# Folding two of five product blocks by accumulating DMAs in a dilated-window attention kernel

## The chip, the cores and the metric

The kernel runs on one core of a Trainium2 chip. The metric is device time in microseconds (us): 264.16 us for the kernel before, the median of 3 runs (264.13 to 264.53). The engines are named as in the profile: PE is TensorE's matmuls and PEld its weight loads, DVE is VectorE, ACT is ScalarE, POOL is GpSimd, SP is SyncE, which only issues DMAs.

## The reference

`x` has 2048 rows of 640 columns, bfloat16. It is normalised (`xn`), and two branches are added to it:

```python
xn = layernorm(x)
return x + A(xn, wqkv, wo) + B(xn, w_gate, w_up, w_down)

# A: 32 heads of 20 columns; each position looks at 8 positions, 2 apart, itself and those before
logits = einsum("bhsd,bhswd->bhsw", q, k[gathered]) * 20 ** -0.5     # masked where position < 0
A = (softmax(logits) applied to v[gathered]) @ wo
# B
B = ((xn @ w_gate) * (xn @ w_up)) @ w_down                            # 1536 columns in the middle
```

## The kernel before

The 2048 positions are cut into 4 chunks of 512, and each chunk into 4 tiles of 128 (16 tiles, t = 4c + q). Per chunk:

- layernorm of the tiles (DVE, and one step `rstd` on POOL, L265), transposes into `xnT` (PE for the first four tiles, DMA transposes on SP's queue for the others, L339);
- `qk` (L396): q and k, transposed (columns on partitions, positions along the free side), as five blocks of 128 of the 640 columns. 25 matmuls for q and 25 for k (L405), ACT copies the results to SBUF (L412);
- `vproj` (L430): v per tile (L438, two halves of 5 matmuls), copied by ACT and stored to `vD` in DRAM by a DMA of POOL's queue (L459);
- `prodlog` (L468): for each of the 8 window positions i, DVE multiplies q by the shifted k (L476, 128 x 2560, all five blocks in one instruction). Two window positions share one tile `pw`. The logits are then sums over the 20 columns of a head, and PE makes them: `Ek` is a matrix of zeros and ones (128 x 32 for each block, as a block holds parts of 7 or 8 heads), and for each block i and window position a matmul of 32 output rows (L492) adds that block's part into PSUM. Four window positions stand beside each other in PSUM partitions. A chunk has two such groups of 4 positions x 5 blocks = 20 matmuls;
- ACT copies the logits to SBUF (L505), SP's queue transposes them (L513, `LT`), DVE and ACT make the softmax (L524 to L546);
- `av` (L574): the v rows of a tile's 8 window positions come from `vD` in one DMA of 1280 KB on SP's queue (L556), DVE multiplies and adds (L581 to L596), and SP's queue transposes the result `o` into `oT` (L603). These v tiles and the `pw` tiles share five buffers (tag `pv`);
- `glu` (L614): 24 groups of 5 matmuls (L623), ACT copies, DVE multiplies into `hT` (L639);
- `down` (L651): 12 matmuls of `hT` by `wd` (L664) and 5 of `oT` by `wo` (L667) per half tile, DVE adds x (L674, tile `xr`, loaded by POOL's queue, L648), and the result is stored by POOL's queue (L698).

The order on each engine is not that of the code. Every piece of work is a step of a plan (`Plan`, L32), with an engine, a cost, dependencies and the time it occupies its engine. `order` (L48) plays these costs through, always taking the ready step with the earliest due time, and the program is emitted in that order; each engine then works in order and waits by semaphore. For a step that is a DMA with a size `kb`, the plan lets it end at the start + 2.0 us (or the end of the one before on that engine) plus kb/340. Two attributes matter here: the logits steps (L496) are `urgent`, taken as soon as they are ready, and have a `margin` of 0.9 us, which is added, with `LAG` = 0.06 us, to the end of what they depend on. So a change of one cost moves steps on all engines.

In the order before, PE takes chunk 0's logits between the v matmuls of tile 4 and those of tiles 5 to 7, chunk 1's between q matmuls of chunk 2, chunk 2's in the down stage of chunk 1, and chunk 3's in the down stage of chunk 2. The last chunk's gate and up matmuls (120, of 25.9 us) and its down stage follow after that.

Of the kernel before, what the change touches and what calls it, by code (L numbers as in the profile page):

```python
# [10 lines left out]
ALU = mybir.AluOpType  # L11
# [20 lines left out]
class Plan:  # L32
# [8 lines left out]
    def add(self, eng, cost, fn, deps=(), occ=None, after=(), kb=0):  # L41
        s = Step(eng, cost, fn, deps, occ, after)
        s.kb = kb
        s.idx = len(self.steps)
        self.steps.append(s)
        return s
# [51 lines left out]
def kernel(  # L98
# [11 lines left out]
    nc = tc.nc  # L110
    P = nc.NUM_PARTITIONS
# [4 lines left out]
    H = 32  # L116
    Dh = D // H
# [5 lines left out]
    KT = D // P  # L123
# [4 lines left out]
    CS = CH * P  # L128
    JL = P // H
    NS = D // 2  # L130
    BF, F32 = dt.bfloat16, dt.float32
    assert D == KT * P and F == FT * P and S == NCH * CS and W * H == 2 * P and Dh == JL * KT

    const = ctx.enter_context(tc.tile_pool(name="const", bufs=1))
# [5 lines left out]
    wq = const.tile([P, KT, D], BF, name="wq")  # L140
    wk = const.tile([P, KT, D], BF, name="wk")
# [4 lines left out]
    wd = const.tile([P, FT, D], BF, name="wd")  # L146
    ident = const.tile([P, P], BF, name="ident")
    mhalf = const.tile([P, 1], F32, name="mhalf")
    Ek = const.tile([P, KT, H], BF, name="Ek")
    negm = const.tile([P, 2, HALO], F32, name="negm")  # L150
    vD = dram.tile([HALO + S, D], BF, name="vD")

# [1 line left out]
    add = plan.add  # L154
    T = {}

    def new(key, shape, dtype, tag, bufs, pool=None):
        t = (pool or sb).tile(shape, dtype, name=tag, tag=tag, bufs=bufs)
        T[key] = t
        return t  # L160
# [10 lines left out]
    def wload(dst, src, eng=None):  # L171
        return lambda: (eng or nc.sync).dma_start(out=dst[:], in_=src.rearrange("(i p) f -> p i f", p=P))
# [31 lines left out]

    def consts_e():
        nc.gpsimd.memset(Ek[:], 1.0)
        nc.gpsimd.affine_select(out=Ek[:], in_=Ek[:], pattern=[[P, KT], [-Dh, H]], compare_op=ALU.is_ge,
                                fill=0.0, base=0, channel_multiplier=1)
        nc.gpsimd.affine_select(out=Ek[:], in_=Ek[:], pattern=[[-P, KT], [Dh, H]], compare_op=ALU.is_ge,
                                fill=0.0, base=Dh - 1, channel_multiplier=-1)  # L210

    def consts_m():
        nc.gpsimd.memset(negm[:], 0.0)
# [95 lines left out]
    def pe_main(cost, fn, deps=(), banks=1):  # L309
        nonlocal main  # L310
        waits = []
        for k in range(banks):
            if len(ring) + k >= 6:
                waits.append(ring[len(ring) + k - 6])
        main = add("PE", cost + 0.165, fn, [main, *waits, *deps], occ=cost)
        return main
# [79 lines left out]
    def qk(c, lo, n, rs=(0, 1)):  # L396
        for r in rs:
            for j in range(KT):
                key = ("qk", c, r, j, lo)

                def pe(i0, i1, key=key, r=r, j=j):
                    if i0 == 0:
                        new(key, [P, 512], F32, "ps", 6, psum)
                    for i in range(i0, i1):
                        nc.tensor.matmul(T[key][:, 0:n], lhsT=(wk if r else wq)[:, i, j * P : (j + 1) * P],  # L405
                                         rhs=T["xnT", c][:, i, lo : lo + n], start=(i == 0), stop=(i == KT - 1))

                def ev(key=key, r=r, j=j):
                    if r == 0 and j == 0 and lo == 0:
                        new(("q", c), [P, KT, CS], BF, "q", 2)  # L410
                    dst = T["k", c][:, j, HALO + lo : HALO + lo + n] if r else T["q", c][:, j, lo : lo + n]
                    nc.scalar.copy(dst, T[key][:, 0:n])  # L412

                one = n / 2400 + 0.0027
                ts = range(c * CH + lo // P, c * CH + (lo + n) // P)
                mine = [WK if r else WQ, *[TX.get(t, TT[t]) for t in ts], LASTPW.get(c - 2)]
                if c or r or j:
                    a = pe_main(KT * one, lambda pe=pe: pe(0, KT), mine + [TT[t] for t in ts])
                else:
                    pe_main(3 * one, lambda pe=pe: pe(0, 3), mine)  # L420
                    a = pe_main(2 * one, lambda pe=pe: pe(3, KT), [TT[t] for t in ts], banks=0)
                e = add("ACT", 0.16 + n / 1200, ev, [a, HALOCP[c]], occ=0.07 + n / 1200)
                ring.append(e)
                (Kk if r else Q).setdefault(c, []).append(e)
# [38 lines left out]


    SPLAST = [None]
    PW, LL, LE, SS, DD, AA, O16, OE, V8, DT = {}, {}, {}, {}, {}, {}, {}, {}, {}, {}

    def prodlog(c):  # L468
        for g in range(2):
            for j in range(4):  # L470
                i = 4 * g + j

                def mul(i=i):
                    if i % 2 == 0:
                        new(("pw", c, i // 2), [P, 2, KT, CS], BF, "pv", 5)
                    nc.vector.tensor_tensor(T["pw", c, i // 2][:, i % 2, :, :], T["q", c][:],  # L476
                                            T["k", c][:, :, DIL * i : DIL * i + CS], ALU.mult)

                m = 8 * c + i
                w = [LL.get(2 * c - 1), O16.get(4 * c - 4), O16.get(4 * c - 3), O16.get(4 * c - 2)][i // 2]  # L480
                PW[m] = add("DVE", 1.48, mul, [*Q[c], *Kk[c], w], occ=1.395, after=[PW.get(m - 1) if i else V8.get(4 * c - 1)])
        LASTPW[c] = PW[m]
        if c == 0:
            load_v8(0)
        for g in range(2):
            n = 2 * c + g

            def lg(g=g):
                l = new(("lps", c, g), [P, 512], F32, "pl", 2, psum)
                for i in range(KT):  # L490
                    for j in range(4):
                        nc.tensor.matmul(l[H * j : H * (j + 1), :], lhsT=Ek[:, i, :], rhs=T["pw", c, 2 * g + j // 2][:, j % 2, i, :],  # L492
                                         start=(i == 0), stop=(i == KT - 1), tile_position=(0, H * j),
                                         skip_group_check=True)

            LL[n] = add("PE", 1.25, lg, [PW[m], LL.get(n - 1), LE.get(n - 2), LE.get(n - 1 - g), CE], occ=1.12)  # L496
            LL[n].urgent = True
            LL[n].margin = 0.9

            def ev(g=g):  # L500
                L = new(("L", c, g), [P, CS], BF, "L", 2)
                if c == 0:
                    ps = T["lps", c, g]
                    nc.vector.tensor_tensor(ps[:, 0:HALO], ps[:, 0:HALO], negm[:, g, :], ALU.add)
                nc.scalar.copy(L[:], T["lps", c, g][:])  # L505

            LE[n] = add("ACT", 0.585, ev, [LL[n], SS.get(n - 2), CM], occ=0.5)

            def tr(g=g):
                if g == 0:  # L510
                    new(("LT", c), [P, CH, W, H], BF, "LT", 1)
                out = T["LT", c][:].rearrange("p t (g w) h -> p t g (w h)", g=2)[:, :, g, :]
                nc.sync.dma_start_transpose(out=out, in_=T["L", c, g][:])  # L513

            early = [SPLAST[0]] if c == 0 else []
            SS[n] = SPLAST[0] = add("SP", 3.5, tr, [LE[n], DD.get(2 * c - 1), DD.get(2 * c - 2)], occ=1.25, after=early, kb=160)

# [32 lines left out]
    def load_v8(t):  # L550
        def fn():
            v = new(("v8", t), [P, W, D], BF, "pv", 5)
            r0 = t * P
            src = vD[r0 : r0 + P, :]
            src = bass.AP(tensor=src.tensor, offset=src.offset, ap=[[D, P], [DIL * D, W], [1, D]])
            nc.sync.dma_start(out=v[:], in_=src)  # L556
        order = [SPLAST[0]] if t < CH - 1 else [SS[2 * (t // CH) + 1]] if t % CH in (1, 2) else []
        c, u = divmod(t, CH)
        order.append(V8[t - 1] if u else PW[8 * c + 6])
        if t == 3:  # L560
            order.append(WL["o"])
        w = LL[2 * c + (u - 1) // 2] if u else O16.get(t - 1)
        V8[t] = add("SP", 6.0, fn, [VS[t], VS.get(t - 1), w, CZ], occ=0.5, after=order, kb=1280)
        if t < 3:
            SPLAST[0] = V8[t]
            V8[t].floor = (40.0, 0, 0)[t]

    def load_down():
        WL["d"] = SPLAST[0] = add("SP", 8, wload(wd, B_w_down), after=[SPLAST[0]], occ=0.5, kb=1920)

    def load_out():
        WL["o"] = SPLAST[0] = add("SP", 8, wo_load, after=[SPLAST[0]], occ=2.7, kb=1100)

# [134 lines left out]
    a = st_in(0, 0)  # L708
    a = st_in(0, 1, a)
    aggr_in(0, a)  # L710
    a = st_in(1, 0)
    a = st_in(1, 1, a)
# [10 lines left out]
    a = st_in(2, 0)  # L723
    a = st_in(2, 1, a)
# [6 lines left out]
    a = st_in(3, 0)  # L731
    a = st_in(3, 1, a)
# [9 lines left out]
    CE = add("POOL", 1.2, consts_e, [C0, RS[3]])  # L742
# [77 lines left out]
```

## Time and profile before

| what | value |
|---|---|
| median of the runs | 264.16 us (264.13 to 264.53) |
| span of the profiled execution | 263.0 us, first to last instruction |
| mean granted TensorE clock | 1.000 |
| logits matmuls, L492 | 160 of 128 x 32 by 128 x 512, 380 ns each in the row, four overlap |
| products, L476 | 32 of 128 x 2560, 1484 ns each |
| DMA moved | 46.55 MB, mean 177 GB/s |

The profile shows one execution, and its own time is given by its span; the runs' times hold what lies around it as well. The page gives busy time by engine, the span in 40 slices (a digit is a tenth of the slice), the DMA queues, the chain of work that ended last, and groups of instructions by line. Further views: an engine's waits in total; the chain in order of time; an engine's timeline (start, duration, line); busy time of each engine in a given stretch, with the DMA share; and DMA issues with the median time from issue to landing. Matmuls overlap in time, so 25 of them of 379 ns take 5.39 us in a row.

### The profile page before, as it was taken

What the parts mean: (1) busy time and instruction counts of PE and PEld (TensorE: products, weight loads), DVE (VectorE), ACT (ScalarE), POOL (GpSimd) and SP (SyncE); (2) the same over time, 40 slices, a digit from 0 to 9 for tenths busy, and PEclk for the clock granted to TensorE, in tenths of its full rate; (3) what the DMA queues carried; (4) which work ended last, traced back from release to release, by engine and by line L of the source; (5) the groups of instructions that cost most, each with busy time, mean ns of one, the idle gap of its engine ahead of it and who ended that gap; (6) DMA issues with size and microseconds to landing.
All of it is one profiled execution on the core that took longest, in us unless ns stands there. A gap on an engine that the chain in (4) does not pass through costs nothing.

```text
span 263.0 us, 4102 instructions
## 1 busy us (share of the span) xinstructions
PE 258.2 (98%) x1574; PEld 140.4 (53%) x1574; DVE 214.6 (82%) x337; ACT 106.1 (40%) x197; POOL 39.4 (15%) x84
## 2 busy tenths in 40 slices
PE   7999999999999999999999999999999999999995
PEld 2645445444577546444477554644456764445763
DVE  5586997999999969999999189999992999993221
ACT  3655557655300258455500155655541105554000
POOL 4551036000031021400001000420000004000000
PEclk9999999999999999999999999999999999999999
DMA  7978997999978139931167299451903995111001
GB/s 217 326 175 231 402 373 171 370 362 244 195 155 270 54 68 370 316 114 27 25 125 250 66 311 319 97 150 25 224 3 75 365 293 134 26 25 25 27 25 50
DMA packets 50707, 46.55 MB, mean 177 GB/s; under 512 B 24786, under 2 KB 47840, under 8 KB 50688
## 3 DMA queue, kind: packets, MB, share of 16 engines
q1 hardware_dynamic: 46704, 37.10, 50.0%
q0 software_dynamic: 2384, 8.05, 9.2%
q10 hardware_dynamic: 1600, 1.15, 1.4%
q8 instruction: 12, 0.20, 0.3%
q14 instruction: 7, 0.06, 0.1%
HBM read 35.39 MB, written 5.26 MB: 155 GB/s over the span
## 4 chain that ended last, share of the span: by engine, by line
PE 94%; DMA 3%; DVE 1%; issue 0%
PE ps L623 39%; PE ps L664 20%; PE ps L405 17%; PE ps L667 8%; PE ps L438 7%; PE pl L492 3%; DMA wq<-in_A_wqkv_dram 3%; DMA x<-in_A_x_dram 1%; DVE st L251 1%; DVE xr L674 0%; DVE mv L257 0%; DVE ve L259 0%; DVE x L270 0%
## 5 line engine op out<-in xcount | busy, mean ns | idle before, releaser
L623 PE MATMUL ps<-xnT,wg 128*128 128x512 bf16 x240 | 59.6, 379 | 0.0
L623 PE MATMUL ps<-xnT,wu 128*128 128x512 bf16 x240 | 59.6, 379 | 0.0
L664 PE MATMUL ps<-wd,hT 128*128 128x320 bf16 (+2 forms) x384 | 57.4, 299 | 0.0
L476 DVE TENSOR_TENSOR pv<-q,k 128x2560 bf16<-128x2560 bf16 x32 | 46.5, 1484 | 1.7 <-ACT k L412 1.7
L664 PEld LDWEIGHTS <-hT 128*128 128x128 bf16 x384 | 37.0, 98 | 16.5 <-issue 0.8
L581 DVE TENSOR_TENSOR pv<-pv,a 128x5120 bf16<-128x5120 bf16 x16 | 45.1, 2819 | 0.1
L628 ACT CAST gs<-ps 128x512 bf16<-128x512 f32 x48 | 28.2, 587 | 32.1 <-PE ps L623 32.1
L623 PEld LDWEIGHTS <-wu 128*128 128x128 bf16 x240 | 23.5, 98 | 28.3
L623 PEld LDWEIGHTS <-wg 128*128 128x128 bf16 x240 | 23.5, 98 | 27.7
L628 ACT CAST us<-ps 128x512 bf16<-128x512 f32 x48 | 28.2, 588 | 22.4 <-PE ps L623 21.4
L674 DVE TENSOR_TENSOR xr<-ps,xr 128x320 bf16<-128x320 f32 (+2 forms) x32 | 15.0, 486 | 24.4 <-PE ps L667 16.1
L667 PE MATMUL ps<-wo,oT 128*128 128x320 bf16 (+2 forms) x160 | 27.0, 299 | 0.0
L698 POOL DMA_DIRECT2D out_dram<-xr x14 | 7.6, 545 | 124.6 <-DVE xr L674 118.0
L590 DVE TENSOR_TENSOR pv<-pv 128x2560 bf16<-128x2560 bf16 x16 | 23.8, 1485 | 0.1
L438 PE MATMUL ps<-wv,xnT 128*128 128x320 bf16 x160 | 23.2, 299 | 0.4 <-ACT xnT L351 0.4
L412 ACT CAST q<-ps 128x512 bf16<-128x512 f32 x20 | 11.7, 586 | 28.3 <-PE ps L405 28.3
L639 DVE TENSOR_TENSOR hT<-gs,us 128x512 bf16<-128x512 bf16 x48 | 19.5, 419 | 4.1 <-ACT us L628 4.1
L405 PE MATMUL ps<-xnT,wq 128*128 128x512 bf16 x100 | 22.4, 379 | 0.4 <-DMA wq<-in_A_wqkv_dram 0.4
L405 PE MATMUL ps<-xnT,wk 128*128 128x512 bf16 x100 | 22.2, 379 | 0.0
L438 PEld LDWEIGHTS <-xnT 128*128 128x128 bf16 x160 | 15.3, 98 | 7.4 <-ACT xnT L351 0.5
L667 PEld LDWEIGHTS <-oT 128*128 128x128 bf16 x160 | 15.5, 98 | 6.3
L251 DVE BATCH_NORM_STATS2 st<-x 128x6 f32<-128x320 bf16 x32 | 13.9, 481 | 4.4 <-DMA x<-in_A_x_dram 4.4
(54 smaller groups left out, 177.4 us busy)
## 6 DMA issues: line engine op xcount, KB each, us to landing
pv<-vD SPq DMA_DIRECT2D x16, 1280.0 KB, 9.9
vD<-v_t POOLq DMA_DIRECT2D x16, 160.0 KB, 4.5
xr<-in_A_x_dram POOLq DMA_DIRECT2D x16, 160.0 KB, 3.6
out_dram<-xr POOLq DMA_DIRECT2D x14, 160.0 KB, 3.7
wg<-in_B_w_gate_dram SPq DMA_DIRECT2D x1, 1920.0 KB, 8.1
wu<-in_B_w_up_dram SPq DMA_DIRECT2D x1, 1920.0 KB, 11.9
wd<-in_B_w_down_dram SPq DMA_DIRECT2D x1, 1920.0 KB, 14.6
x<-in_A_x_dram SPq DMA_DIRECT2D x11, 160.0 KB, 6.8
```

Source lines behind the costliest of these rows:

```text
L251: nc.vector.bn_stats(T["st", t][:, g, :], T["x", t][:, g * NS : (g + 1) * NS])
L405: nc.tensor.matmul(T[key][:, 0:n], lhsT=(wk if r else wq)[:, i, j * P : (j + 1) * P], rhs=T["xnT", c][:, i, lo : lo + n], start=(i == 0), ...
L438: nc.tensor.matmul(T["psv", t, n][:, 0:NS], lhsT=T["xnT", c][:, i, q * P : (q + 1) * P], rhs=wv[:, i, n * NS : (n + 1) * NS], start=(i == ...
L476: nc.vector.tensor_tensor(T["pw", c, i // 2][:, i % 2, :, :], T["q", c][:], T["k", c][:, :, DIL * i : DIL * i + CS], ALU.mult)
L581: nc.vector.tensor_tensor(v[:].rearrange("p w (j h) -> p w j h", j=Dh, h=H), v[:].rearrange("p w (j h) -> p w j h", j=Dh, h=H), T["a", n][ ...
L590: nc.vector.tensor_tensor(v[:, 0:4, :], v[:, 0:4, :], v[:, 4:8, :], ALU.add)
L623: nc.tensor.matmul(ps[:], lhsT=(wu if r else wg)[:, i, f * P : (f + 1) * P], rhs=T["xnT", c][:, i, :], start=(i == 0), stop=(i == KT - 1))
L628: nc.scalar.copy(s[:], T[key][:])
L639: nc.vector.tensor_tensor(h[:], T["gs", c, f][:], T["us", c, f][:], ALU.mult)
L664: nc.tensor.matmul(ps, lhsT=T["hT", c, f][:, q * P : (q + 1) * P], rhs=wd[:, f, sl], start=(f == 0), stop=(f == FT - 1 and not wo_part))
L667: nc.tensor.matmul(ps, lhsT=T["oT", t][:, g, :], rhs=wo[:, g, sl], start=False, stop=(g == KT - 1 and f1 == FT))
L674: nc.vector.tensor_tensor(T["xr", t][:, sl], T["psD", t, n][:, 0:w], T["xr", t][:, sl], ALU.add)
```

## The change

The columns of q and k are taken in another order: block j now holds the columns j, j + 5, j + 10 and so on of the 640. As a head has 20 columns and 20 is a multiple of 5, each block holds 4 columns of every head, and partition p belongs to head p // 4 in each of the five blocks. The weights themselves stay as loaded: PE's weight load reads every fifth column. `Ek` becomes one matrix of 128 x 32 for all blocks.

Since a partition has the same head in every block, blocks may be added to each other before the logits. After every second product a new step `fold` does so: POOL issues a DMA with an accumulating destination, which adds the blocks 2 and 3 of a `pw` tile (2 positions x 2 blocks x 512, 512 KB) into its blocks 0 and 1. The logits then sum the blocks 0, 1 and 4: 12 matmuls a group, not 20, and they wait for the folds. The product steps, the softmax and all else keep their code; the order is planned anew.

```diff
-    Ek = const.tile([P, KT, H], BF, name="Ek")
+    Ek = const.tile([P, H], BF, name="Ek")
...
-                        nc.tensor.matmul(T[key][:, 0:n], lhsT=(wk if r else wq)[:, i, j * P : (j + 1) * P],
+                        nc.tensor.matmul(T[key][:, 0:n], lhsT=(wk if r else wq)[:, i, :].rearrange("p (c b) -> p c b", b=KT)[:, :, j],
...
+    LEVELS = (1, 1, 1, 1)
+    FOLDER = ('POOL', 'POOL', 'POOL', 'POOL')
+    LEFT = (tuple(range(KT)), (0, 1, KT - 1), (0, KT - 1), (0,))
+    HALVES = ((0, 2, 2, 4), (0, 1, 1, 2), (0, 1, KT - 1, KT))
+
+    def fold(c, u):
+        s = PW[8 * c + 2 * u + 1]
+        for lo, hi, a, b in HALVES[: LEVELS[c]]:
+            def fn(lo=lo, hi=hi, a=a, b=b):
+                w = T["pw", c, u]
+                if FOLDER[c] == "DVE":
+                    nc.vector.tensor_tensor(w[:, :, lo:hi, :], w[:, :, lo:hi, :], w[:, :, a:b, :], ALU.add)
+                else:
+                    nc.gpsimd.dma_start(out=w[:, :, lo:hi, :], in_=w[:, :, a:b, :], accum_op=ALU.add)
+            n = (hi - lo) * 2 * CS
+            if FOLDER[c] == "DVE":
+                s = add("DVE", 0.25 + n / 1920, fn, [s], occ=0.165 + n / 1920)
+            else:
+                s = add("POOL", 4.0, fn, [s], occ=1.2, kb=n / 4)
+        return s
...
+                if i % 2:
+                    FO[4 * c + i // 2] = fold(c, i // 2)
...
-                for i in range(KT):
+                left = LEFT[LEVELS[c]]
+                for i in left:
                     for j in range(4):
-                        nc.tensor.matmul(l[H * j : H * (j + 1), :], lhsT=Ek[:, i, :], rhs=T["pw", c, 2 * g + j // 2][:, j % 2, i, :],
-                                         start=(i == 0), stop=(i == KT - 1), tile_position=(0, H * j),
+                        nc.tensor.matmul(l[H * j : H * (j + 1), :], lhsT=Ek[:], rhs=T["pw", c, 2 * g + j // 2][:, j % 2, i, :],
+                                         start=(i == left[0]), stop=(i == left[-1]), tile_position=(0, H * j),
                                          skip_group_check=True)
 
-            LL[n] = add("PE", 1.25, lg, [PW[m], LL.get(n - 1), LE.get(n - 2), LE.get(n - 1 - g), CE], occ=1.12)
+            took = 0.022 + 0.2195 * len(LEFT[LEVELS[c]])
+            LL[n] = add("PE", took + 0.13, lg, [*[FO[4 * c + u] for u in range(4)], LL.get(n - 1), LE.get(n - 2), LE.get(n - 1 - g), CE], occ=took)
```

In the order that the plan makes of it, chunk 0's logits stand 25 v matmuls later on PE than before, chunk 1's behind all q and k matmuls of chunk 2, chunk 2's between the k matmuls of chunk 3, and chunk 3's behind the first 5 gate matmuls of the last chunk. PE has 64 matmuls fewer, POOL's queue 16 DMAs more. On DVE, chunk 0's products follow each other as before; in the other chunks they mix with other `xr` and `hT` steps than before.

More of the change, by code (lines that the diff above doesn't have):

```diff
@@ L206, in consts_e @@
         nc.gpsimd.memset(Ek[:], 1.0)
-        nc.gpsimd.affine_select(out=Ek[:], in_=Ek[:], pattern=[[P, KT], [-Dh, H]], compare_op=ALU.is_ge,
+        nc.gpsimd.affine_select(out=Ek[:], in_=Ek[:], pattern=[[-JL, H]], compare_op=ALU.is_ge,
                                 fill=0.0, base=0, channel_multiplier=1)
-        nc.gpsimd.affine_select(out=Ek[:], in_=Ek[:], pattern=[[-P, KT], [Dh, H]], compare_op=ALU.is_ge,
-                                fill=0.0, base=Dh - 1, channel_multiplier=-1)
+        nc.gpsimd.affine_select(out=Ek[:], in_=Ek[:], pattern=[[JL, H]], compare_op=ALU.is_ge,
+                                fill=0.0, base=JL - 1, channel_multiplier=-1)
     def consts_m():
@@ L465 @@
     SPLAST = [None]
+    FO = {}
     PW, LL, LE, SS, DD, AA, O16, OE, V8, DT = {}, {}, {}, {}, {}, {}, {}, {}, {}, {}
+    LEVELS = (1, 1, 1, 1)
[17 more added lines that the diff above has]
+        return s
     def prodlog(c):
```

## The prediction

> **What bounds the kernel now.** I read the engine table and the slices first, then TensorE's waits, then the chain of waits in order of time.
>
> ```profile
> PE 258.2 (98%) x1574; PEld 140.4 (53%) x1574; DVE 214.6 (82%) x337; ACT 106.1 (40%) x197; POOL 39.4 (15%) x84
> ...
> PE   7999999999999999999999999999999999999995
> ...
> DMA  7978997999978139931167299451903995111001
> ```
>
> PE is busy in every slice; DVE at 82% is not the limit. PE's waits add up to 2.1 us, all before 12.3 us:
>
> ```profile
> PE ps L242 <- DVE wv L192: 1.3, 1, 1.3
> PE ps L405 <- DMA wq<-in_A_wqkv_dram: 0.4, 1, 0.4
> PE ps L438 <- ACT xnT L351: 0.4, 1, 0.4
> ```
>
> So from 12.23 us to the end the span is a sum of matmuls in a fixed order: a matmul removed comes off one for one, and a new wait in that row goes on one for one. The logits (L492) stand in the chain four times (start, duration):
>
> ```profile
> 35.34 1.36 PE ps L438 x10
> 36.70 2.27 PE pl L492 x40
> 38.97 4.18 PE ps L438 x30
> ...
> 91.85 2.27 PE pl L492 x40
> ...
> 145.89 2.27 PE pl L492 x40
> ...
> 197.05 2.27 PE pl L492 x40
> ```
>
> **1. Matmuls removed: minus 3.6 us.** A chunk's 40 logits matmuls take 2.27 us, 0.057 each; 24 take 1.36. Saved 0.91 in each of 4 chunks, all on the path: 3.6 us.
>
> **2. Strided weight loads: 0.** The 200 loads for q and k now read every fifth column. Such a load shows 98 ns (L405, PEld), beside matmuls that follow each other every 216 ns (25 take 5.39 us). 118 ns may be added before it shows. No row has a strided load: from below nothing can be gained, from above see rival C. I take 0.
>
> **3. The later place of the logits: 0.** In the changed order, chunk 3's logits stand behind the first five gate matmuls of the last chunk, not in the down stage before it. Counted in matmuls of the trace, they end at 213.2 us instead of 199.3. Before, the last `o` (tile 15) ended on DVE at 237.2, 37.8 us after the logits. In between the new order has three more hT products (0.34 each) and six fewer xr additions (0.40): 36.4 us, so 249.6, plus 2.8 for the transpose: 252.4. PE would need it at 254.5 (the old 258.2 less 3.6). 2 us of slack; without them it would be PE's wait, one for one.
>
> **4. The accumulating DMAs.** After every second product GpSimd issues one: 512 KB read from blocks 2 and 3, added into 0 and 1. 16 in all, and the logits wait for them. Products and adds stay as they were on DVE. On POOL's queue an issue is bounded by the 0.55 us of today's issues and twice that, as there are twice the rows (256 of 2 KB, not 128); I take 1.1, by the row count. Behind chunk 0's four stand a vD store and the rstd of tiles 8 and later; the four issues end near 36.3, and before, that store was issued at 37.46, the rstd at 38.02. Nothing is pushed. In chunks 1 to 3 they alternate with stores to out that nobody waits for at once. SP's queue issues nothing new, but its transfers share the DMA engines.
>
> The place that matters is chunk 0. DVE's timeline first, then busy time by stretch (its last two columns are the DMA share and GB/s):
>
> ```profile
> 23.85 11.31 DVE L476 TENSOR_TENSOR pv<-q,k 128x2560 bf16<-128x2560 bf16 x8 [1.68 <-ACT k L412]
> ```
>
> ```profile
> 34.00:36.00 2.00, 2.00 (x14) 1.07 (x12) 2.00 (x4) 1.17 (x3) 0.00 (x0) 1.00 1.02 386
> 36.00:38.00 2.00, 2.00 (x34) 1.01 (x35) 1.93 (x8) 1.00 (x3) 0.54 (x1) 1.00 1.08 365
> 38.00:40.00 2.00, 2.00 (x28) 1.06 (x21) 1.97 (x9) 1.21 (x3) 1.79 (x4) 1.00 0.79 267
> ```
>
> Eight products in 11.31 us: a pair every 2.83, ready at 26.7, 29.5, 32.3 and 35.2. Meanwhile the DMA engines are full (share 1.02 or more from 24 to 38) with wu and the first v load from vD, and free at about 38.5. PE, with 25 more v matmuls (0.136 each) ahead of the logits, reaches them at 36.7 + 3.4 = 40.1, and the half that needs the last two adds at 40.8: 5.6 us after the last product.
>
> What does one add cost the DMA engines? No row shows an accumulating DMA. 512 KB at the 394 to 405 GB/s of 24 to 38 us is 1.3 us as a copy, the lower end. An add must also read its destination: twice the reads make 2.6, and if reads and writes all counted, 3.9, the upper end. [...]
>
> [...]
>
> How such a transfer shares full engines is shown by POOL's own: four xr loads issued together at 44.4, beside SP's loads, and the same four at 219.5, alone:
>
> ```profile
> xr<-in_A_x_dram POOLq DMA_DIRECT2D x4, 160.0 KB, 6.2
> ```
> ```profile
> xr<-in_A_x_dram POOLq DMA_DIRECT2D x4, 160.0 KB, 3.0
> ```
>
> Half as fast: about an equal share. A single 160 KB issue lands after 5.3 us in the full stretch (vD at 25.3) and 2.1 in an idle one (out at 89.6).
>
> Neither side is idle until the work is done, so the sum decides: SP's backlog ended at 38.5; four adds of 2.6 make 10.4 more, so all ends by 48.9. At an equal share from 29.5 (the first add's data) the adds end about there too; with somewhat more than half, at 47.6. PE therefore waits from 40.8 to about 48.3: **7.5 us** (6.8 to 8.1). At 3.9 the sum ends at 54.1: 13.3 us. Behind the waiting matmul stand all of PE's work and, through it, everything else; wu (needed 1 us after the logits) has landed by then, at 43 to 45.
>
> Before the opening matmuls TensorE was idle, and these ten (L242) take 4.45 us, about 0.42 apart against 0.216 later: a cold start loses 2 us. An idle 7.5 us may bring it again: 0 to 2.2, I take 1.5, nearer the one row there is.
>
> **Chunks 1 to 3.** The DMA share is 0.11 to 0.26 from 84 to 96 us. Alone, an add lands after 2.1 (the 160 KB row), less its 0.4 of data, plus 0.5 for the longer issue and 2.6: 4.8. The plan releases the logits 2.0 + 512/340 + 0.06 + 0.9 = 4.5 us after the last product, PE is up to one group (1.1) later, and the half that needs the last add 0.7 after that: 5.2 to 6.3. No wait; at 3.9, up to 0.9 each. The first adds of chunks 2 and 3 overlap a v load (6.8 us, issued at 137.3 before), which may push the last: 0 to 1.5. I take 0.5 in all.
>
> **Sum.** 263.0 - 3.6 + 7.5 + 1.5 + 0.5 = 268.9 us of span. The median of the runs is 264.16, 1.16 above the profiled span: **270.0 us**, 2.2% slower. Less than 0.2% can't be told from no change here.
>
> **Rivals.**
> - **B, the adds run like copies (faster).** At 1.3 us each, four take 5.2 and keep pace with the pairs at half share (2.6 against 2.83). The last lands between 35.2 + 3.5 (idle engines: 2.1 + 0.9 data + 0.5) and 35.2 + 7.1 (the 5.3 row plus 352 KB at half rate): a wait of 0 to 1.5, say 0.8. 263.0 - 3.6 + 0.8 + 1.16 = 261.4 (260.6 to 262.1). For it: nothing measured here says that adding costs more. Against it: the destination must be read. The point between B and my forecast: the logits' wait reaches 3.6 us, at adds of about 1.8 to 2.0 us.
> - **C, the strided loads show.** Beyond 216 ns each ns costs 0.2 us over 200 loads; at three times 98 it is 15.6, so 276 even with B. For it: 10 bytes between columns is new. Against it: 118 ns of cover. [...]
> - **D, in between:** adds of 1.6 to 2.2 us, or more than half a share for POOL: waits of 2 to 5.5, no or little cold start: 262.6 to 267.5, on either side of no change.
>
> **Chances.** Forecast 0.52 (its own range 267.5 to 274.5, with the wait from 6 to 10 and the cold start from 0 to 2.2; adds of 3.9 us would give 277 and are left out); B 0.30; C 0.05; D 0.13. My range reaches from B to the forecast's upper end: 260.9 to 274.5. Faster: B and a little of D, 0.33. Within 0.2%: 0.05. Slower: 0.62.
>
> **What would show it.** PE's waits: a new row "PE pl <- DMA pv<-pv" of about 7.5 us, almost all in chunk 0; in B it is under 1.5. The DMA issues: pv<-pv lands after 4.8 us or so alone, and 9 or more at its longest. L405's weight loads: still 98 ns, or hidden under 216. The chain: 24 logits matmuls in 1.36 us. DVE's last `o` well ahead of PE. It is wrong if the adds land within 5.6 us in chunk 0, or if the wait sits in chunks 1 to 3.

## The result and the profile after

The changed kernel takes 281.96 us, the median of 4 runs (280.57 to 283.04), beside 264.33 (264.13 to 264.53) for the kernel before: a ratio of 1.0664, interval 1.0628 to 1.0701. It is slower by three times what was forecast (270.0), and outside the range (260.9 to 274.5). The profiled execution took 280.57 us, with a span of 278.8. In the experiments below, times, ranges and ratios are of the undisturbed runs; a few runs of e5, e7, e10, e11 and e12 in a slower state (in e12 one of 269.77 us at a mean clock of 0.987, beside a median of 264.82) are left out.

The page of the changed kernel: busy time, TensorE's slices, its granted clock, the DMA engines, POOL's queue (packets, MB, share of 16 engines' span), and the adds from issue to landing.

```profile
PE 260.0 (93%) x1510; PEld 143.5 (51%) x1510; DVE 214.8 (77%) x337; ACT 104.8 (38%) x197; POOL 58.4 (21%) x100
...
PE   7999971999999998999999997999999959999996
...
PEclk9999995799999999999999999999999997999999
DMA  7979999699996997895046995991115997940122
...
q0 software_dynamic: 6736, 16.44, 25.4%
...
pv<-pv POOLq DMA_DIRECT2D x16, 512.0 KB, 7.8
```

PE was busy in every slice before; now it has four holes, one for each chunk, and behind the first and the last the clock is down too (digits 5 and 7 of PEclk, and 7). PE's waits in total (us, times, longest):

```profile
PE pl L517 <- DMA pv<-pv: 14.1, 7, 3.8
PE ps L242 <- DVE wv L192: 1.3, 1, 1.3
PE ps L438 <- ACT xnT L351: 0.4, 1, 0.4
```

One row is new, the one that the prediction named: logits that wait for an add. It holds 14.1 us, and not "almost all in chunk 0". PE's timeline has the seven (start, duration; in brackets the idle time before it):

```profile
39.34 0.39 PE L517 MATMUL pl<-pv,Ek 128*32 128x512 bf16 x2
41.23 0.82 PE L517 MATMUL pl<-pv,Ek 128*32 128x512 bf16 x10 [1.50 <-DMA pv<-pv]
44.89 0.61 PE L517 MATMUL pl<-pv,Ek 128*32 128x512 bf16 x2 [2.83 <-DMA pv<-pv]
49.32 1.46 PE L517 MATMUL pl<-pv,Ek 128*32 128x512 bf16 x10 [3.82 <-DMA pv<-pv]
...
107.63 1.04 PE L517 MATMUL pl<-pv,Ek 128*32 128x512 bf16 x14
109.55 0.82 PE L517 MATMUL pl<-pv,Ek 128*32 128x512 bf16 x10 [0.88 <-DMA pv<-pv]
...
166.69 1.04 PE L517 MATMUL pl<-pv,Ek 128*32 128x512 bf16 x14
169.59 0.82 PE L517 MATMUL pl<-pv,Ek 128*32 128x512 bf16 x10 [1.86 <-DMA pv<-pv]
...
225.68 0.83 PE L517 MATMUL pl<-pv,Ek 128*32 128x512 bf16 x12
226.85 0.39 PE L517 MATMUL pl<-pv,Ek 128*32 128x512 bf16 x2 [0.34 <-DMA pv<-pv]
230.14 1.44 PE L517 MATMUL pl<-pv,Ek 128*32 128x512 bf16 x10 [2.90 <-DMA pv<-pv]
```

A group's ten last matmuls take 0.82 us in chunks 1 and 2, but 1.46 and 1.44 in chunks 0 and 3, at a lowered clock (0.50 granted from 48 to 52 us, 0.57 from 230 to 234). From the first logits matmul of a chunk to the start of the next other work, less the 1.36 us that 24 matmuls need, PE lost 10.0, 1.3, 2.3 and 4.5 us; the matmuls behind chunks 0 and 3, still at the low clock, lost 1.1 and 1.0 more. That is 11.1 + 1.3 + 2.3 + 5.5 = 20.2. With 3.6 removed and a start that was 0.7 earlier (the first logits would have come at 40.0 by the matmuls ahead of them, and came at 39.3), 263.0 + 20.2 - 3.6 - 0.7 = 278.9, beside a span of 278.8: nothing else grew.

### The profile page after: what moved, and what is told of

It reads as the page before. It is cut to its first block, busy times and chain, and to the rows that moved or that the text cites. A ratio compares the mean times of both kernels' runs of the same rounds, so it can differ in the third digit from the quotient of the medians.

```text
span 278.8 us, 4033 instructions
## 1 busy us (share of the span) xinstructions
PE 260.0 (93%) x1510; PEld 143.5 (51%) x1510; DVE 214.8 (77%) x337; ACT 104.8 (38%) x197; POOL 58.4 (21%) x100
## 3 DMA queue, kind: packets, MB, share of 16 engines
q0 software_dynamic: 6736, 16.44, 25.4%
## 4 chain that ended last, share of the span: by engine, by line
DVE 31%; PE 25%; issue 23%; DMA 13%; POOL 5%; ACT 2%; POOLq 0%; DVEq 0%; ACTq 0%
PE ps L649 11%; DMA pv<-pv 8%; DVE pv L607 8%; DVE pv L498 6%; PE ps L690 5%; DVE pv L616 5%; DMA vD<-v_t 4%; PE ps L405 4%; POOL pv L482 3%; DVE hT L665 3%; DVE pv L620 2%; PE ps L438 2%; PE ps L693 2%; DVE xr L700 2%; DVE st L251 1%
## 5 line engine op out<-in xcount | busy, mean ns | idle before, releaser
L649 PE MATMUL ps<-xnT,wu 128*128 128x512 bf16 x240 | 60.7, 384 | 0.0
L498 DVE TENSOR_TENSOR pv<-q,k 128x2560 bf16<-128x2560 bf16 x32 | 46.2, 1481 | 1.7 <-ACT k L412 1.7
L607 DVE TENSOR_TENSOR pv<-pv,a 128x5120 bf16<-128x5120 bf16 x16 | 45.1, 2818 | 0.1
L482 POOL DMA_DIRECT2D pv<-pv x16 | 19.1, 1195 | 48.3 <-issue 25.4
L724 POOL DMA_DIRECT2D out_dram<-xr x14 | 10.3, 737 | 77.4 <-DVE xr L700 77.4
L438 PE MATMUL ps<-wv,xnT 128*128 128x320 bf16 x160 | 23.9, 304 | 0.4 <-ACT xnT L351 0.4
L517 PE MATMUL pl<-pv,Ek 128*32 128x512 bf16 x96 | 9.7, 437 | 14.1 <-DMA pv<-pv 14.1
L444 ACT CAST v_t<-ps 128x320 bf16<-128x320 f32 x32 | 13.2, 429 | 21.7 <-DMA vD<-v_t 17.8
L438 PEld LDWEIGHTS <-xnT 128*128 128x128 bf16 x160 | 15.4, 99 | 8.2 <-issue 1.3
## 6 DMA issues: line engine op xcount, KB each, us to landing
wu<-in_B_w_up_dram SPq DMA_DIRECT2D x1, 1920.0 KB, 17.1
```

The costliest lines, as they stand in the source:

```text
L438: nc.tensor.matmul(T["psv", t, n][:, 0:NS], lhsT=T["xnT", c][:, i, q * P : (q + 1) * P], rhs=wv[:, i, n * NS : (n + 1) * NS], start=(i == ...
L444: nc.scalar.copy(T["v_t", t][:].rearrange("p (j h) -> p j h", j=Dh, h=H)[:, :, n * H // 2 : (n + 1) * H // 2], T["psv", t, n][:, 0:NS].rea ...
L482: nc.gpsimd.dma_start(out=w[:, :, lo:hi, :], in_=w[:, :, a:b, :], accum_op=ALU.add)
L607: nc.vector.tensor_tensor(v[:].rearrange("p w (j h) -> p w j h", j=Dh, h=H), v[:].rearrange("p w (j h) -> p w j h", j=Dh, h=H), T["a", n][ ...
L649: nc.tensor.matmul(ps[:], lhsT=(wu if r else wg)[:, i, f * P : (f + 1) * P], rhs=T["xnT", c][:, i, :], start=(i == 0), stop=(i == KT - 1))
```

## The experiments

Theory after the result: the adding DMAs are the whole loss. Each takes the 16 DMA engines some 2.9 us, they land late, and PE stands. Rivals: the strided weight loads; POOL's issues; other loads beside the adds; the place of the logits in the order; the vector engine (DVE) close behind PE.

### The strided loads, and chunk 0

```diff
-    LEVELS = (1, 1, 1, 1)
+    LEVELS = (0, 0, 0, 0)      # e1_permute_only
+    LEVELS = (0, 1, 1, 1)      # e2_no_fold_chunk0
```

> Only the permuted columns and the one Ek: no block is added to another, the logits sum five blocks as before (LEVELS all 0). Theory: the strided weight loads hide under the 216 ns between matmuls, so this is the kernel before, 264.2 to 264.6 us, and L405's loads still show about 98 ns. Rival (strided loads show): each ns beyond 216 costs 0.2 us; part of the 17.6 us would sit here, 266 or more.

Measured: 264.16 us (264.05 to 264.79), before 264.16; ratio 1.0002, interval 0.9992 to 1.0011. The permuted columns and the single `Ek` cost nothing. A strided load is slower by itself, here in the changed kernel (98 ns before), but 118 ns are still hidden beside matmuls that come every 216:

```profile
L405 PEld LDWEIGHTS <-wk 128*128 128x128 bf16 x100 | 11.7, 118 | 10.1 <-issue 0.4
```

> No adds in chunk 0 (LEVELS 0, 1, 1, 1), all else as in the changed kernel. Theory (adds queue behind each other and behind SP's loads; the waits belong to their chunks): the 11.1 us that chunk 0 loses on PE (10.0 in the wait, 1.1 of slow matmuls after it) go, the 0.9 us saved there come back: 282.0 - 10.2 = 271.8, and PE's waits in chunks 1 to 3 stay at 1.3, 2.3 and 5.5. Rival (the waits of chunks 1 to 3 hang on the delay of chunk 0): they change by more than 1 us each.

Measured: 269.26 us (267.56 to 270.02), ratio 1.0183 (1.0145 to 1.022). Chunk 0's four adds, with the order that goes with them, are worth 12.7 us of the 17.6. Those of the other chunks are dearer than the 0.5 us forecast: with them alone the kernel is 5.1 us slower than before, though 2.7 us of matmuls are gone. The theory's 271.8 was missed, for the waits did not stay: they are 0.8 us in chunk 1, 2.6 in chunk 2 and none in chunk 3, where the new order brings PE to the logits 6.5 us after the last product, and not 5.4.

### Copies instead of adds, and both by themselves

```diff
-                    nc.gpsimd.dma_start(out=w[:, :, lo:hi, :], in_=w[:, :, a:b, :], accum_op=ALU.add)
+                    nc.gpsimd.dma_start(out=w[:, :, lo:hi, :], in_=w[:, :, a:b, :])      # e3_copy
```

> The 16 DMAs copy blocks 2 and 3 over 0 and 1 in place of adding to them: same queue, rows, bytes written and order, but no read of the destination; the output is not the reference's. Theory (the second read makes an add cost about twice a copy): the q0 queue takes some 1.3 us of all engines for each instead of 2.9, chunk 0's last one lands before 43, PE waits less than 3 us in all: 261.4 to 264. Rival (what costs is the issue on POOL's queue, with its 256 rows and its latency): copies land as late as adds, 279 to 283.

Measured: 266.58 us (265.82 to 267.04), ratio 1.0087 (1.0067 to 1.0107). The queue of POOL and the wait at the logits in this run:

```profile
q0 software_dynamic: 4688, 16.44, 17.1%
```
```profile
PE pl L517 <- DMA pv<-pv: 1.6, 1, 1.6
```

The megabytes are the same 16.44 as with adds, the share of the engines is 17.1% of 264.0 us and not 25.4% of 278.8. Less the 24.2 us of the kernel before (9.2% of 263.0), a copy takes (45.1 - 24.2) / 16 = 1.3 us of all engines, an add (70.8 - 24.2) / 16 = 2.9. Same order, same number of issues, 15.4 us apart. The last copy of chunk 0 had landed by 42.1 us, as the theory had it; its time, 261.4 to 264, was missed, and e9 below shows why. POOL's own part differs by 0.5 us an issue (0.72 and 1.20); the engines' part differs by 1.6 us each, 6.4 in a chunk. It is the adding, and not the issue, that costs.

> The DMAs by themselves on idle engines, nothing of the model computed: one add, another, four adds in a row, the same with copies of POOL's queue, then with copies of SP's queue; x is copied to the output. Theory: four adds land 2.1 to 2.9 us apart and four copies 1.2 to 1.5 apart; a single add lands after 4.5 to 5.5 us, a single copy after 3.3 to 4. Rival (issue bound): adds and copies in a row both land 1.2 us apart, as POOL issues them.

A program with nothing of the kernel but such DMAs, on idle engines: one add twice, four adds, one copy twice, four copies, and the copies again from SP's queue. L27 on DVE reads each tile as soon as it has landed, so its starts show the landings:

```profile
24.18 1.36 POOL L36 DMA_DIRECT2D pw<-pw  x1 [23.74 <-DVE pw L27]
29.46 1.80 DVE L27 COPY pw<-pw 128x128 bf16<-128x128 bf16 x8 [5.59 <-DMA pw<-pw]
...
46.62 0.20 DVE L27 COPY pw<-pw 128x128 bf16<-128x128 bf16 x1 [8.62 <-DMA pw<-pw]
49.33 0.19 DVE L27 COPY pw<-pw 128x128 bf16<-128x128 bf16 x1 [2.52 <-DMA pw<-pw]
52.03 1.34 DVE L27 COPY pw<-pw 128x128 bf16<-128x128 bf16 x6 [2.50 <-DMA pw<-pw]
...
53.67 0.75 POOL L39 DMA_DIRECT2D pw<-pw  x1 [10.51 <-DVE pw L27]
56.90 1.80 DVE L27 COPY pw<-pw 128x128 bf16<-128x128 bf16 x8 [3.53 <-DMA pw<-pw]
...
68.75 0.19 DVE L27 COPY pw<-pw 128x128 bf16<-128x128 bf16 x1 [5.20 <-DMA pw<-pw]
70.15 0.20 DVE L27 COPY pw<-pw 128x128 bf16<-128x128 bf16 x1 [1.21 <-DMA pw<-pw]
71.87 1.34 DVE L27 COPY pw<-pw 128x128 bf16<-128x128 bf16 x6 [1.52 <-DMA pw<-pw]
```

Alone, an add is there 5.3 us after its issue began (29.46 - 24.18), a copy after 3.2. In a row adds land 2.7 us apart, copies 1.4 and 1.7, from SP's queue as from POOL's; as POOL issues an add every 1.2 us, the issue is not the bound. An add costs 2.7 / 1.56 = 1.7 copies in a row, and 2.9 / 1.3 = 2.2 by engine time in the kernel. That the read of the destination makes it dearer is not shown here: in the kernel's queue an add also counts 272 packets and a copy 144, and no run separates the two.

### The place of the logits, and the load of v beside the adds

```diff
-                s = add("POOL", 4.0, fn, [s], occ=1.2, kb=n / 4)
+                s = add("POOL", 4.0, fn, [s], occ=1.2, kb=n / 2)      # e5_honest_price
+                s.floor = (41, 42, 46, 50)[u] if c == 0 else 0
...
-            LL[n].margin = 0.9
+            LL[n].margin = 2.4
```

> The planner is told what the adds cost here: 1024 KB of queue time each (3.0 us) instead of 512 KB, 2.4 us of margin ahead of the logits instead of 0.9, and for chunk 0 ends of 41, 42, 46 and 50 us. It then puts 48.7 us of other matmuls ahead of chunk 0's logits instead of 35.1, and 213.4 us instead of 202.6 ahead of the last logits. Theory 1 (the loss is only PE standing at logits that were placed too early): the four waits of 20.2 us go, the 3.6 us of removed matmuls show, 260 to 264 us. Theory 2 (the add stands in a loop of each chunk that the vector engine already fills, products to logits to softmax to products, so a later place only moves the idle time to another wait or to the end): PE waits of at least 8 us stay, at the logits of chunks 1 to 3, at the down projection or at the end, 268 to 280 us. I hold theory 2 for likelier.

Measured: 294.28 us (291.85 to 295.62), 1.114 times the kernel before. PE's waits:

```profile
PE ps L691 <- DVE hT L666: 10.8, 4, 4.0
PE ps L694 <- DMA wo<-in_A_wo_dram: 6.0, 1, 6.0
PE ps L691 <- DVE o L623: 2.5, 1, 2.5
...
PE pl L518 <- DMA pv<-pv: 0.6, 1, 0.6
```

Theory 2 holds in its mechanism, beyond its range of 268 to 280: the logits hardly wait, and much behind them does. The allowances were generous (chunk 0's logits came at 59.7 us and had no wait at all), so the size of the loss is this plan's own; that the wait moved and did not go is what it shows.

```diff
+            if t % CH == 0 and t:      # e6_v_after_adds; in e14_v_after_adds_0: if t == 0, and pw of chunk 0
+                nc.sync.dma_start(out=scr[:], in_=T["pw", t // CH, 3][0:1, 1, 0:2, 0:2])
             nc.sync.dma_start(out=v[:], in_=src)
...
-        order.append(V8[t - 1] if u else PW[8 * c + 6])
+        order.append(V8[t - 1] if u else PW[8 * c + 6] if c == 0 else FO[4 * c + 3])      # e14: if c else FO[3]
```

The plan is told of it too; the order on PE, DVE, ACT and POOL stays that of the changed kernel, and in e6 that on SP changes.

> In chunks 1 to 3 the first load of v (1280 KB) is held back by a transfer of four elements that reads the last added product, so that it starts only when the four adds have landed. Theory A (the adds of chunks 1 to 3 land late since they share the 16 DMA engines with that load): the last adds land 5 to 6 us after their issue, the waits of chunks 2 and 3 fall from 2.3 and 5.5 us to about 1.5 each, 276 to 279 us. Theory B (the adds are late by their own time, issue and engines, and by the products being finished late): the waits stay, 281 to 283 us, or more if the late load of v makes the weighting wait.

Measured: 290.24 us (288.25 to 290.51), ratio 1.0971 (1.0945 to 1.0998). At the logits of chunks 1 to 3 PE waited 0.90, 1.98 and 1.95 us, not 0.88, 1.86 and 3.24: theory B for chunks 1 and 2, theory A for a part of chunk 3 only.

```profile
110.11 0.82 PE L518 MATMUL pl<-pv,Ek 128*32 128x512 bf16 x10 [0.90 <-DMA pv<-pv]
...
174.54 0.82 PE L518 MATMUL pl<-pv,Ek 128*32 128x512 bf16 x10 [1.98 <-DMA pv<-pv]
...
235.67 0.82 PE L518 MATMUL pl<-pv,Ek 128*32 128x512 bf16 x10 [1.95 <-DMA pv<-pv]
```

The late load costs more than it brings; a new row has 7.6 us:

```profile
PE pl L518 <- DMA pv<-pv: 13.2, 6, 4.2
PE ps L693 <- DVE hT L668: 7.6, 5, 2.8
```

> In chunk 0 alone the first load of v (1280 KB) is held back, by a transfer of four elements that reads the last added product, until the four adds have landed; all else as in the changed kernel. Theory (the adds of chunk 0 share the 16 DMA engines with this load, which a window of 400 GB/s moves in 3.4 us, and with the load of the up weights): PE resumes some 2 to 3 us earlier, 278 to 280 us. Rival (the adds and the up weights alone fill the engines until 49 us, the load of v takes its turn behind them): 281 to 283 us.

Measured: 285.17 us (284.04 to 286.43), ratio 1.0793 (1.0757 to 1.0829). In chunk 0 the theory was right: the last ten logits matmuls started at 46.17 and not at 49.32, so 3 us of that wait were the v load's share. At the end it was wrong, as was the rival's number. The first weighting by the softmax (L610, L607 in the changed kernel) began at 60.6 us, beside 61.5: the late load gave back most of the 3 us. Chunk 1's last add landed at 109.2, beside 109.6, and PE, which was there earlier, waited 2.6 us for it and got the low clock behind that (0.57 from 110 to 114 us). PE's earlier start became a longer wait, and the same followed in chunk 2: waits of 0.86 and 2.17 us, with the low clock behind them (digit 5 of PEclk from 171 to 178 us, and ten matmuls in 1.47 us, not 0.82).

### The adds on DVE

```diff
-    FOLDER = ('POOL', 'POOL', 'POOL', 'POOL')
+    FOLDER = ('DVE', 'DVE', 'DVE', 'DVE')      # e7_dve; with LEVELS (1, 1, 1, 0) e10, (1, 1, 0, 0) e11, (1, 0, 0, 0) e12
```

> The same sums by 16 adds on the vector engine instead of 16 DMAs; about 1.2 us each by the 1.48 us that a product of 2560 elements a partition takes, 19 us in all on an engine that is busy for 215 us. The logits keep three blocks. Theory 1 (the loss is the DMA's latency and its share of the DMA engines; the vector engine has 50 us of slack): no wait at the logits, 260 to 264 us. Theory 2 (the vector engine's loop is what sets when logits can be had, slack or not): most of the 19 us show at the end, 270 to 280 us.

Measured: 268.14 us (267.86 to 269.02), ratio 1.0159 (1.0144 to 1.0174); between the two theories. An add takes 1.22 us (DVE's L480), and nothing waits at the logits. PE waits in the last down stage instead, 22.5 and 28.7 us behind the start of the last logits:

```profile
PE ps L690 <- DVE hT L665: 5.1, 2, 2.8
```

> Adds on the vector engine in chunks 0, 1 and 2, none in chunk 3, whose logits keep five blocks. The planner puts 203.7 us of other matmuls ahead of the last logits, 210.2 in the version with adds in every chunk. Theory (with the adds on the vector engine nothing waits at the logits, and what cost time was the tail behind the last logits): three times 0.91 us is gained, 260.3 to 262 us. Rival (the adds fill the vector engine's loop in every chunk, and it is this that shows at the end): 264.5 to 268 us.

> Adds on the vector engine in chunks 0 and 1 only; 196.9 us of other matmuls ahead of the last logits (185.1 in the kernel before). Theory of the tail: twice 0.91 us is gained, 262.0 to 262.8 us. Rival of the loop: 263.5 to 266 us.

> Adds on the vector engine in chunk 0 only; 190.0 us of other matmuls ahead of the last logits. Theory of the tail: 0.91 us is gained, 263.0 to 263.5 us. Rival of the loop: 264 to 265 us.

Measured: 264.87 us (ratio 1.0052, 1.0024 to 1.008), 264.69 (1.0020, 0.9995 to 1.0044) and 264.82 (1.0033, 1.0015 to 1.0051). The theory of the tail fell: with the last chunk's adds left out none is faster than before, and the 0.9 us a chunk are not to be seen. For e10 and e12 that is the loop's forecast; in e11 the interval reaches to no change. The profile of e10, taken at 268.03 us and so above its median, has PE waiting 3.5 us for `oT` in chunk 0's down stage, which DVE's `o` feeds. That of e12, at 264.78 us, has the same wait with 1.0 us, as much as the 0.9 us of matmuls that this run leaves out.

### What the removed matmuls are worth

```diff
-                    nc.gpsimd.dma_start(out=w[:, :, lo:hi, :], in_=w[:, :, a:b, :], accum_op=ALU.add)
+                    pass      # e9_no_adds
```
```diff
-    LEVELS = (1, 1, 1, 1)
+    LEVELS = (0, 0, 0, 0)      # e13_old_order
...
-                left = LEFT[LEVELS[c]]
+                left = LEFT[1]
```

> The sixteen adding DMAs are left out and nothing is put in their place; the order of every other instruction is that of the changed kernel, with three blocks of logits (so the sums of blocks 2 and 3 are missing from the output). What this costs against the kernel before is the price of the later places in the order alone. Theory (place costs nothing, all of the loss is made by the adding DMAs): 263.0 - 3.6 = 259.4 us of span, 259.5 to 261 us with what lies around it. Rival (the order that the planner makes for the adds, with 17.5 us more of other matmuls ahead of the last logits, costs time by itself): 262 to 266 us, with waits at the down projection or at the end.

Measured: 264.37 us (263.56 to 265.71), ratio 1.0012 (0.9995 to 1.0029). The rival was right: with 64 matmuls fewer and no adds at all nothing is gained. PE's waits beyond the 2 us that all kernels have at the start:

```profile
PE ps L690 <- DVE hT L665: 1.7, 3, 1.0
```

> The order of every instruction is that of the kernel before (31.7, 84.5, 136.2 and 185.1 us of other matmuls ahead of the four logits); no adds, and three blocks in the logits instead of five, so that the sums of blocks 2 and 3 are missing from the output. It shows what the 64 removed matmuls are worth by themselves. Theory (PE is the bound, and the later places of the order with adds cost the 3.6 us that were missed there): 259.4 us of span, 260.3 to 261.5 us. Rival (the vector engine's loop stands so close behind PE that a faster PE waits for it whatever the order): 262.5 to 264.5 us, with PE waits at the down projection.

Measured: 261.06 us (260.62 to 261.58), ratio 0.988 (0.9862 to 0.9898), and no wait of PE behind 7 us. So PE is the bound as long as the order is the old one, and the order that the plan makes for the adds costs 3.3 us by itself. In e9 the work from chunk 0's logits to chunk 1's took 58.1 us for 55.9 us of matmuls; nearly all of the excess lies at the start of the down stage, around waits for `hT` of 0.21 and 1.05 us. There 46 matmuls take 8.3 us (67.3 to 75.6), and 6.25 in the kernel before (68.9 to 75.1):

```profile
73.24 2.55 PE L690 MATMUL ps<-wd,hT 128*128 128x320 bf16 x16 [1.05 <-DVE hT L665]
```

The loss is now a ladder of kernels that differ in one thing each (medians, us):

| step | time | difference |
|---|---|---|
| before; and with permuted columns (e1) | 264.16; 264.16 | 0.0 |
| 64 matmuls fewer, old order (e13) | 261.06 | -3.1 |
| the order planned for the adds (e9) | 264.37 | +3.3 |
| 16 copies on POOL's queue (e3) | 266.58 | +2.2 |
| adds in place of copies (the change) | 281.96 | +15.4 |

### Adds that land in time

```diff
-    LEVELS = (1, 1, 1, 1)
+    LEVELS = ((0, 0), (1, 0), (1, 0), (1, 0))      # e8_early_pairs: by half of the logits
+    LEVELS = ((0, 0, 0, 0), (1, 0, 0, 0), (1, 0, 0, 0), (1, 0, 0, 0))      # e15_first_pair: by pair
+    LEVELS = ((0, 0), (0, 1), (0, 1), (0, 1))      # e16_added_last, with
+    SEQ = (4, 5, 6, 7, 0, 1, 2, 3)                 # products in this order
...
```

> Only the first two pairs of products of chunks 1 to 3 are added, by DMA; the last two, and all of chunk 0, keep five blocks. 24 of the logits matmuls are left out, 3 x 0.455 = 1.4 us of PE. The adds that remain are issued 6 us or more ahead of the logits. Theory (a DMA add costs nothing if it is issued more than its own 5.3 to 8 us before PE needs it, beside its share of the DMA engines): no wait at the logits, 262.6 to 263.2 us, against 264.2 before. Rival (any add takes so much of the DMA engines that other transfers land late, or that the pairs arrive late all the same): 264.5 to 267 us.

Measured: 264.98 us (264.06 to 266.99), ratio 1.003 (1.0013 to 1.0048). The rival's range, and its mechanism: the order of PE is the old one, but in chunks 1 and 3 the second add came 0.8 us late, and with the restart (0.4 us, by 3.0 less 1.84 and the wait of 0.76 to 0.78) the logits took 3.0 us there, 0.7 more than before; in chunk 2 they took 1.84, 0.43 less. Twice plus 0.7 and once minus 0.4 make 1.0 (the start was 0.3 earlier): the span went from 263.0 to 263.8.

> Only the first pair of products of chunks 1 to 3 is added by DMA, issued some 10 us ahead of the logits; the other three pairs, and all of chunk 0, keep five blocks, and the order of PE is that of the kernel before. 12 logits matmuls are left out, 0.68 us of PE by 2.27 us for 40. Theory (an add that lands in time costs nothing, and PE, which is the bound, gives the whole 0.68 us): 263.3 to 263.6 us. Rival (even three adds, by their share of the DMA engines, make other transfers late by as much): 264.0 to 264.8 us.

Measured: 264.16 us (264.08 to 264.81), ratio 0.9996 (0.9985 to 1.0008). No wait at the logits, and no gain: my 0.68 us were not there. The number is the rival's, but no transfer was late; the cause is another. The same chunk's logits in e15 and, with whole groups of four left out, in e8:

```profile
91.55 2.34 PE L519 MATMUL pl<-pv,Ek 128*32 128x512 bf16 x36
```
```profile
146.30 1.91 PE L517 MATMUL pl<-pv,Ek 128*32 128x512 bf16 x32
```

40 take 2.34 us in this view as well. The matmuls of the four column groups overlap, 379 ns each and 0.057 us apart on average; where two of four were left out, no time came off (36 in 2.34 us), and where all four were, it did (32 in 1.91). A matmul at 0.057 us is a quarter of a group at 0.227, and only whole groups came off. What e15 does show is that three adds which land in time cost nothing.

> In every chunk the products of the second half of the logits are now made first, and in chunks 1 to 3 these two pairs are added by DMA; the logits of the first half (five blocks) stand on PE ahead of those of the second (three blocks), so that the adds have 1.1 us more than in the version with the early pairs, where the second add came 0.8 us late. 24 logits matmuls are left out in whole groups of four, 0.45 us a chunk by the 1.84 us that 32 took there against 2.27 for 40. Theory (PE gives the whole gain where no wait and hardly a new order stands against it): 263.0 - 1.3 = 261.7 us of span, 262.7 to 263.3 us. Rival (the adds land later still when PE needs them later, or the small shift of the last logits, 187.1 instead of 185.1 us of other matmuls ahead of them, costs the gain): 264.0 to 265.5 us.

Measured: 263.02 us (262.80 to 263.35), before 264.11 (264.04 to 264.47); ratio 0.9956, interval 0.9942 to 0.9969. The theory holds: with whole groups left out and the adds given 1.1 us more, no row of PE's waits names an add, and the chunk's 32 matmuls stand in one piece:

```profile
91.34 1.91 PE L518 MATMUL pl<-pv,Ek 128*32 128x512 bf16 x32
```

This version beats both kernels, by 0.4% against the one before: 1.1 us of the 1.3 that three times 0.43 make.

## Why the prediction was wrong, step by step

| step | forecast | measured |
|---|---|---|
| 1, matmuls removed | -3.6 | 24 in 1.36 us, -3.1 at the end (e13) |
| 2, strided loads | 0 | 0 (e1); 118 ns a load, not 98 |
| 3, later place of the logits | 0 | 0 in the changed kernel; 3.3 without its waits (e9 against e13) |
| 4, chunk 0: wait and cold start | 7.5 + 1.5 | 10.0 + 1.1 |
| 4, chunks 1 to 3 | 0.5 | 9.1 (1.3, 2.3, 5.5) |

**What bounds the kernel** was right: e13 gives back nearly all of the removed matmuls, and each wait in PE's row went on one for one.

**The failed step is "Chunks 1 to 3. ... No wait"**, a term of 0.5 us that measures 9.1. Its two sides: PE needs the last add 5.2 to 6.3 us after the last product, I said, and it lands after 4.8. The first side held nearly. The last products end at 103.5, 162.8 and 221.8 us (DVE's L498), and PE is ready for their sums at 108.7, 167.7 and 227.2 (the starts above less the idle time): 5.2, 4.9 and 5.4 us, in chunk 2 a little less than I said. The second side did not hold. The adds land 6.1, 6.8 and 8.3 us after the products. They don't fly alone, as I had them: the DMA share that I read there, 0.11 to 0.26, was that of the kernel before at 84 to 96 us, and the adds themselves, with the v load that starts at the first products, fill the engines. Changed kernel, chunk 3 (the last three columns: granted clock, DMA share, GB/s):

```profile
216.00:220.00 4.00, 4.00 (x31) 2.88 (x30) 4.00 (x5) 0.00 (x0) 1.99 (x3) 1.00 1.08 267
220.00:224.00 4.00, 4.00 (x32) 2.88 (x30) 2.74 (x5) 0.00 (x0) 2.08 (x3) 1.00 1.12 225
224.00:228.00 4.00, 2.90 (x24) 1.07 (x22) 0.49 (x1) 1.17 (x2) 1.59 (x3) 1.00 1.12 227
```

Four adds of 2.9 us are 11.6 us of engines, in the 11.9 us in which chunk 3's products are made; there is no room for 1280 KB of v. Even alone (5.3 us, and 0.3 from product to issue) the last add would have been late by 0.2 to 0.7 us. I had weighed the sum of the work against the engines in chunk 0 and not in the other three. e6 takes the v load away and finds 1.3 us of it in chunk 3 and nothing in chunks 1 and 2, so there it is the adds' own length, one behind another: with copies in their place (e3) these chunks have no wait at the logits. What chunk 3 lost beyond its 3.2 us of waits is the low clock (0.57 granted from 230 to 234 us; 0.6 us in its last ten matmuls, 1.0 behind them) and, by difference, 0.7 us of restart.

**Chunk 0 was right in mechanism and 2 us short.** The add's price was forecast at 2.6 us of the engines, twice a copy's 1.3, which was my estimate: no run shows why it should be twice, and the runs give 2.9 (2.7 in the run of its own); the adds end at 49.3, not 48.3, and PE is there at 39.3, not 40.1. e14 shows that of this wait 3 us are the share of the v load, whose bytes were in the backlog that I counted. The cold start was forecast at 1.5; it cost 1.1 behind the logits and 0.6 in their last ten matmuls (1.46 us for 0.82), which are part of the 10.0. So the price of the restart was nearly right, and the wait was too short.

**Step 3 looked in the wrong place.** I followed the last `o` to the end of chunk 3. What is late first, in e9, is `hT` in chunk 0's down stage. In the changed kernel this doesn't show, since PE stands at the logits anyway and DVE catches up; e9 shows that it would have taken the gain if the adds had been free. So rival B would not have given 261.4 us: with copies it is 266.6.

**Two slips changed nothing.** The rows from 24 to 38 us have 365 to 415 GB/s, 394 in the mean, and not 394 to 405; a copy stays at 1.3 us. Rival C on top of rival B's 261.4 would be 277.0, not 276.

**Open**: which of DVE's steps the plan should move so that later logits don't make `hT` late; why adds on DVE in the early chunks alone bring nothing, beyond the wait for `oT` in e12; and whether an add is dear by its second read or by its packets.

## What to carry to other kernels

Price a DMA that adds at about twice a copy's engine time (1.7 to 2.2 times here), and count that time in every stage where it is issued against all else that the DMA engines move there; a landing time from an idle stretch is no price for four in a row (5.3 us alone; 6.1 to 8.3 from the last product in chunks 1 to 3). On PE, full here (98%) and working in order, work handed to another engine paid only where its result was there before the old order needed it: moving the consumer back moved the wait to the next stage (e5, 294.28 us; e9, 264.37 without any add), and taking the add only where it had slack (e16, 263.02) was the one version with adds that won. Of matmuls that overlap in column groups, only whole groups came off (36 in 2.34 us, as 40; 32 in 1.91).

## What the runs showed of the hardware

A wait of PE can cost more than its length: behind chunk 0's, the matmuls at the low clock lost another 1.1 us. In the changed kernel the granted clock stays 1.00 behind the waits of 0.88 and 1.86 us and falls among those of chunk 0 (clock, DMA share and GB/s at the end of each line):

```profile
42.00:44.00 2.00, 0.06 (x2) 0.00 (x0) 0.53 (x2) 0.00 (x0) 0.00 (x0) 0.62 1.10 240
...
48.00:50.00 2.00, 0.68 (x8) 0.29 (x10) 0.00 (x0) 0.09 (x1) 0.00 (x0) 0.50 1.02 395
50.00:52.00 2.00, 2.00 (x11) 0.73 (x6) 0.18 (x1) 1.41 (x3) 0.00 (x0) 0.50 0.29 106
```

e14, with one wait of 2.58 us in chunk 1, has 0.57 in the 4 us behind it:

```profile
110.00:114.00 4.00, 4.00 (x18) 2.37 (x19) 0.76 (x4) 1.86 (x4) 0.62 (x1) 0.57 0.35 67
```

In e5 it is 0.50 behind a wait of 2.29 us, but in e6 it stays at full behind one of 2.36 us (the wait, then the stretch behind it; e5 first):

```profile
43.74 2.21 PE L650 MATMUL ps<-xnT,wu 128*128 128x512 bf16 x5 [2.29 <-DMA wu<-in_B_w_up_dram]
...
44.00:46.00 2.00, 2.00 (x6) 0.76 (x5) 0.00 (x0) 0.00 (x0) 0.00 (x0) 0.50 1.11 245
```
```profile
147.34 0.31 PE L693 MATMUL ps<-wd,hT 128*128 128x320 bf16 x1 [2.36 <-DVE hT L668]
...
148.00:150.00 2.00, 2.00 (x17) 1.44 (x15) 1.97 (x4) 0.00 (x0) 0.00 (x0) 1.00 0.00 0
```

So the length of the wait alone doesn't decide: one of 2.29 us was enough in e5, one of 2.36 us in e6 was not. What decides is not shown. For the way back, 0.57 over 4 us in e14 makes about 3.4 us at a clock of 0.50, by estimate, if the low clock there was the 0.50 that the changed kernel and e5 show.
